# Attention, a dense MoE and a routed MoE on one core: joint attention bursts, earlier weight requests, another order of the last routing, and VectorE on both weight halves of three experts

## Chip, core and metric

The kernel runs on one core of a Trainium2 chip. The metric is the device time of one execution in microseconds; the median of the runs is compared. The inputs are drawn at random from a fixed seed.

## What is computed

Three stages follow each other. `x` passes from one to the next.

```
# 1. chunked attention, 4 x 8 heads, 768 positions, head size 64; per chunk of 32 positions
k_full = concat(mem_k (8), k[16 left .. 8 right]);  v_full likewise
out[chunk] = softmax(q[chunk] @ k_full.T / 8) @ v_full
# 2. dense MoE block on 3072 tokens of 512
g = x @ w_gate;  x = (silu(g) * (x @ w_val)) @ w_out          # 512 -> 1536 -> 512
# 3. routed MoE, 8 experts, top 1
e = argmax(x @ w_gate2);  p = softmax(x @ w_gate2)[e];  o = sigmoid(x @ w_output_gate)[e]
out = p * o * (relu(x @ w1[e]) @ w2[e])                       # 512 -> 1024 -> 512
```

The dense weights of stage 2 come as 64-bit floats and are converted on the chip; the rest is 32-bit.

## The kernel before

**Tiles.** The 3072 tokens are 8 token groups of 384. A token group is 6 attention tiles of 64 positions (48 tiles in all). A program counter, not a scheduler, sets the order: the order in which the code is written is the order of each engine's queue.

**Attention as pieces.** `attention_pieces` lists small steps: `at_T` transposes queries or keys of a tile, `at_S` scores one tile, `at_S2` scores two tiles (from tile 14, `PAIRED`, on), `at_N` normalises, `at_PT` transposes probabilities, `at_PV` multiplies with the values of one tile and writes `xh` and its remainder `xl`. The pieces of token group g+1 are spread over the 36 slots of token group g (`slot`, `run_pieces`). Most pieces take a buffer of the PSUM pool `ps_a`, a ring of three.

**The dense block.** For each of 12 column blocks f of a token group, TensorE does 12 matmuls for the gate (`m1_gate`), 12 for the value (`m1_val`) and 9 for the output of the block before (`m1_out`). Every operand is split in a high and a low part, which gives three passes for each product. `split_gv` and `split_o` make the parts of the weights for each token group anew: ScalarE copies the high one, GpSimd subtracts for the low one.

**Conversion.** In token group 0 the 36 weight pieces of 512 KB are loaded on SyncE's queue into `wst`, and converted by two ScalarE steps (`conv_act`), three VectorE steps and a GpSimd add (`conv_dve`). Seven are begun in the attention of token group 0, the others about one in a slot. `wst` has two buffers of three pieces each, and `conv_rest` asks for the piece three ahead.

**Routing.** After a token group `m1_done` puts its routing steps in a list with delays in slots (`later`, `tick`): `rt_T` transposes, `rt_L` logits, `rt_M` and `rt_1` the choice, `rt_2` the positions, `rt_3` the write of the rows, `rt_R` the scatter of token numbers into a table by GpSimd. The last token group also makes the schedule of the experts, 14 steps of very small VectorE work, one in each tick.

**Experts.** Steps 0 to 2 (`NEARLY`) serve three experts with 256 tokens each, steps 3 on are read from the schedule. Each step has 8 chunks of hidden columns: `mm1` (12 matmuls), relu on ScalarE and its remainder `h` on VectorE, `mm2` one chunk later. `split_chunk` splits the two weights of a chunk two chunks ahead: ScalarE copies both high parts, VectorE subtracts for the first weight, GpSimd for the second. There are two ticks in a chunk. Rows of tokens are gathered by GpSimd (`gather`) with indices that SyncE reads from the table (`load_idx`).

## Time and profile before

| | |
|---|---|
| median of 3 runs | 1137.72 us (1136.55 to 1138.33) |
| the profiled execution | 1136.55 us, span 1134.8 us |
| TensorE busy | 1088.2 us, 96% |
| VectorE, ScalarE, GpSimd busy | 607.1, 595.6 and 667.7 us |
| chain that ended last | TensorE 82%, VectorE 6%, DMA 3%, GpSimd 3% |

The span is that of the profiler's records, and 1.75 us lie around it. Busy shares are averages over stages with different limits: attention of token group 0 up to 42 us, token groups 0 to 7 up to 788 us, then the experts. A busy TensorE says little by itself, since a matmul that starts late inside a run of matmuls is also counted.

### The profile page before, as it was taken

The numbers are of one execution on the slowest core, as the hardware profiler recorded it, in microseconds if no ns is written. First come the engines' busy times: TensorE is split into PE (matmuls) and PEld (weight loads), VectorE is DVE, ScalarE is ACT, GpSimd is POOL, SyncE is SP. The second block draws the span as 40 slices with busy tenths as digits, with TensorE's granted clock in tenths as the row PEclk, the third lists the DMA queues.
The fourth block names the chain that finished last, engine by engine and source line by source line (L and its number), as shares of the span: only waits on it lengthen the run. The fifth ranks groups of instructions, "written<-read, shape, count | busy, mean of one in ns | idle before, by whom it ended". The sixth has DMA issues, their size and how long they took to land.

```text
span 1134.8 us, 20274 instructions
## 1 busy us (share of the span) xinstructions
PE 1088.2 (96%) x7268; PEld 967.5 (85%) x7268; DVE 607.1 (53%) x1260; ACT 595.6 (52%) x1336; POOL 667.7 (59%) x459
## 2 busy tenths in 40 slices
PE   7889899999999999999999999999989999999994
PEld 5778788898898999889889899998769988888883
DVE  6799954544444544544444443334786344444563
ACT  5678755545556555555554554444535344445551
POOL 4589854554654554464455465566547566666773
PEclk7799999999999999999999999999999999999997
DMA  8776624301211220221130010254319655555774
GB/s 218 191 201 206 180 69 123 54 22 36 65 38 38 59 46 23 59 44 31 45 59 22 8 42 1 75 104 149 120 54 336 226 175 179 187 173 192 223 233 127
DMA packets 204574, 125.73 MB, mean 111 GB/s; under 512 B 110768, under 2 KB 181552, under 8 KB 204466
## 3 DMA queue, kind: packets, MB, share of 16 engines
q1 hardware_dynamic: 199282, 110.70, 35.6%
q0 software_dynamic: 5184, 13.66, 3.5%
q8 instruction: 59, 0.97, 0.4%
q14 instruction: 49, 0.40, 0.1%
HBM read 110.82 MB, written 14.04 MB: 110 GB/s over the span
## 4 chain that ended last, share of the span: by engine, by line
PE 82%; DVE 6%; DMA 3%; POOL 3%; issue 2%; ACT 2%; SPq 0%; POOLq 0%; ACTq 0%; DVEq 0%
PE ps_g L533 33%; PE acc L574 16%; PE g L1036 12%; PE o L1071 11%; PE ps_pv L436 2%; PE ps_t L328 2%; PE ps_att L419 2%; PE ps_att L389 1%; DMA st<-in_moe_w_gate_dram 1%; DMA st<-in_moe_w_val_dram 1%; PE ps_x L620 1%; PE a L1022 1%; POOL gvl L183 1%; DVE ps_c L231 1%; DVE ps_c L229 1%
## 5 line engine op out<-in xcount | busy, mean ns | idle before, releaser
L183 POOL TENSOR_TENSOR gvl<-w,gvh 128x1024 fp32r<-128x1024 f32 x96 | 233.6, 2434 | 89.2 <-ACT gvh L182 60.6
L533 PE MATMUL ps_g<-xh,gvh 128*128 128x384 f32 x768 | 270.3, 352 | 0.6 <-ACT gvh L182 0.6
L533 PE MATMUL ps_g<-xh,gvl 128*128 128x384 f32 x768 | 259.5, 338 | 2.4 <-POOL gvl L183 2.4
L533 PE MATMUL ps_g<-xl,gvh 128*128 128x384 f32 x768 | 259.4, 338 | 0.0
L183 POOL TENSOR_TENSOR ol<-w,oh 128x512 fp32r<-128x512 f32 x96 | 124.4, 1295 | 197.6 <-ACT oh L182 197.5
L574 PE MATMUL acc<-oh,h 128*128 128x512 f32 x576 | 202.0, 405 | 0.0
L546 DVE SCALAR_TENSOR_TENSOR th<-th,ps_g 128x384 f32<-128x384 f32 x96 | 53.0, 552 | 185.8 <-ACT th L541 183.1
L533 PEld LDWEIGHTS ps_g<-xh,gvh 128*128 128x128 f32 x768 | 144.9, 189 | 5.2 <-ACT gvh L182 0.8
L533 PEld LDWEIGHTS ps_g<-xh,gvl 128*128 128x128 f32 x768 | 144.6, 188 | 3.5 <-POOL gvl L183 3.5
L533 PEld LDWEIGHTS ps_g<-xl,gvh 128*128 128x128 f32 x768 | 145.1, 189 | 1.9
L557 ACT CAST h<-th 128x384 fp32r<-128x384 f32 x96 | 49.2, 512 | 165.6 <-DVE th L555 165.5
L574 PEld LDWEIGHTS acc<-oh,h 128*128 128x128 f32 x576 | 108.2, 188 | 27.6 <-issue 4.4
L574 PE MATMUL acc<-ol,h 128*128 128x512 f32 x288 | 113.8, 395 | 0.3 <-POOL ol L183 0.3
L1046 ACT ACTIVATE h<-g 128x256 fp32r<-128x256 f32 (+2 forms) x96 | 36.0, 375 | 146.2 <-PE g L1036 134.0
L563 DVE TENSOR_TENSOR h<-th,h 128x384 fp32r<-128x384 f32 x96 | 82.8, 862 | 40.0 <-ACT h L557 40.0
L182 ACT CAST gvh<-w 128x1024 fp32r<-128x1024 f32 x96 | 100.4, 1047 | 1.9 <-POOL w L237 1.8
L541 ACT ACTIVATE th<-ps_g 128x384 f32<-128x384 f32 x96 | 47.0, 489 | 91.2 <-PE ps_g L533 91.0
L1048 DVE SCALAR_TENSOR_TENSOR h<-g,h 128x256 fp32r<-128x256 f32 (+2 forms) x96 | 39.4, 410 | 95.5 <-ACT h L1046 41.5
L555 DVE TENSOR_TENSOR th<-th,ps_g 128x384 f32<-128x384 f32 x96 | 53.0, 552 | 58.2 <-PE ps_g L533 56.5
L972 POOL TENSOR_TENSOR wl<-w,wh 128x512 fp32r<-128x512 f32 x30 | 49.4, 1648 | 35.4 <-ACT wh L970 32.2
L1071 PE MATMUL o<-gvh,h 128*128 128x512 f32 x184 | 66.3, 399 | 4.1 <-DVE h L1048 4.1
L972 POOL TENSOR_TENSOR gvl<-w,gvh 128x512 fp32r<-128x512 f32 x30 | 46.9, 1563 | 37.8 <-ACT gvh L970 36.3
(252 smaller groups left out, 2344.3 us busy)
## 6 DMA issues: line engine op xcount, KB each, us to landing
w<-in_moe_w_dram SPq DMA_DIRECT2D x120, 256.0 KB
ra<-in_moe_w_dram SPq DMA_DIRECT2D x72, 256.0 KB
kt<-in_k_dram SPq DMA_DIRECT2D x35, 176.0 KB
vt<-in_v_dram SPq DMA_DIRECT2D x35, 176.0 KB
xs<-xr SPq DMA_DIRECT2D x8, 769.5 KB
st<-in_moe_w_gate_dram SPq DMA_DIRECT2D x12, 512.0 KB
st<-in_moe_w_val_dram SPq DMA_DIRECT2D x12, 512.0 KB
st<-in_moe_w_out_dram SPq DMA_DIRECT2D x12, 512.0 KB
```

The costliest lines, as they stand in the source:

```text
L182: nc.scalar.copy(out=hi, in_=src)
L183: lo_eng.tensor_tensor(out=lo, in0=src, in1=hi.bitcast(F32), op=ALU.subtract)
L533: nc.tensor.matmul(ps, a[:, c], x[:, kk, :], start=(n == 0), stop=(n == 3 * KD - 1))
L541: nc.scalar.activation(out=th, in_=ps, func=AF.Tanh, scale=0.5)
L546: nc.vector.scalar_tensor_tensor(out=th, in0=th, scalar=1.0, in1=ps, op0=ALU.add, op1=ALU.mult)
L555: nc.vector.tensor_tensor(out=hh, in0=hh, in1=ps, op=ALU.mult)
L557: nc.scalar.copy(out=h1, in_=hh)
L563: nc.vector.tensor_tensor(out=h2, in0=hh, in1=h1.bitcast(F32), op=ALU.subtract)
L574: nc.tensor.matmul(accs[g][j], a[:, c], w_, start=(f == 0 and n == 0), stop=(f == NF - 1 and n == 2))
L972: eng.tensor_tensor(out=b[:, i], in0=r[:, i], in1=a[:, i].bitcast(F32), op=ALU.subtract)
L1036: nc.tensor.matmul(ps, wx[:, 0, c * P:(c + 1) * P], xx[:, c, :], start=(i == 0), stop=(i == 3 * KD - 1))
L1071: nc.tensor.matmul(ysd[s][t][0:hx.shape[1]], hx, wx[:, 1], start=(j == 0 and i == 0), stop=(j == NFE - 1 and i == len(passes) - 1))
```

## The change

There are five edits.

- Loads: `wst` has six buffers of one piece each, and from the second conversion on `conv_rest` asks for the piece five ahead.
- Attention: the values of two tiles are multiplied in one piece (`at_PV2`), and from tile 12 on together with the scores of the next two tiles (`at_PVS`). Mask and exponentials of the second of these tiles are a piece of their own (`at_X`). The transposes of tile 6 move from the attention ahead of token group 0 into its slots.
- Routing: the steps get other delays, in successive slots for the last two token groups, and later ones for the others. The schedule's 14 steps come at ticks 10 to 29 instead of 13 to 26.
- A memset of one number for each partition goes ahead of each of the last token group's three scatters.
- For the 24 chunks of the first three experts VectorE does both subtractions of a split.

```diff
@@ -91,7 +92,7 @@
     s_wst = ctx.enter_context(ExitStack())
     ldp = s_att.enter_context(tc.tile_pool(name="ldp", bufs=2))
     ap2 = s_att.enter_context(tc.tile_pool(name="ap2", bufs=2))
-    wst = s_wst.enter_context(tc.tile_pool(name="wst", bufs=2, side="right"))
+    wst = s_wst.enter_context(tc.tile_pool(name="wst", bufs=NST, side="right"))
...
         if W64:
-            dst, cast = staged[f].rearrange("p c t -> p (c t)"), lambda a: a.bitcast(I32)
+            staged[f, j] = wst.tile([P, KD * P, 2], I32, tag="st", name="st")
+            dst, cast = staged[f, j].rearrange("p c t -> p (c t)"), lambda a: a.bitcast(I32)
         else:
-            dst, cast = wres[f], lambda a: a
-        n = KD * P * (2 if W64 else 1)
-        dst = dst[:, j * n:(j + 1) * n]
+            dst, cast = wres[f][:, j * KD * P:(j + 1) * KD * P], lambda a: a
...
-        st = staged[f][:, j * KD * P:(j + 1) * KD * P, :]
+        st = staged.pop((f, j))
...
     def conv_rest():
         nonlocal n_conv
-        if n_conv >= 3:
-            load_w(*divmod(n_conv + 3, 3))
+        if n_conv > 0:
+            load_w(*divmod(n_conv + NST - 1, 3))
         conv_dve()
         n_conv += 1
...
         for z in range(2):
-            s = ap2.tile([P, HP, CTXM], F32, tag="s", name="s", bufs=3)
-            mx = sm.tile([P, HP, 1], F32, tag="mx", name="mx")
-            nc.vector.tensor_tensor(out=s, in0=ps[z], in1=mk, op=ALU.add)
-            nc.vector.tensor_reduce(out=mx, in_=s, axis=AX.X, op=ALU.max, negate=True)
-            den = dens[(i + z) % 3]
-            for j in range(HP):
-                nc.scalar.activation(
-                    out=s[:, j, :], in_=s[:, j, :], func=AF.Exp,
-                    bias=mx[:, j, :], accum_out=den[:, j, 0:1])
-            probs[i + z] = (s, den)
+            score[i + z] = ps[z]
+
+    def at_X(i):
+        t = i % NT // 2 * 2
+        mi = 3 if t == 0 else (4 if t == NT - 2 else 0)
+        mk = masks[:, mi:mi + 1, :].to_broadcast([P, HP, CTXM])
+        s = ap2.tile([P, HP, CTXM], F32, tag="s", name="s", bufs=3)
+        mx = sm.tile([P, HP, 1], F32, tag="mx", name="mx")
+        nc.vector.tensor_tensor(out=s, in0=score.pop(i), in1=mk, op=ALU.add)
+        nc.vector.tensor_reduce(out=mx, in_=s, axis=AX.X, op=ALU.max, negate=True)
+        den = dens[i % 3]
+        for j in range(HP):
+            nc.scalar.activation(
+                out=s[:, j, :], in_=s[:, j, :], func=AF.Exp,
+                bias=mx[:, j, :], accum_out=den[:, j, 0:1])
+        probs[i] = (s, den)
...
+    def at_PV2(i):
+        g, tt = divmod(i, GU)
+        if g not in xT:
+            xT[g] = (xp.tile([P, KD, GT], F32R, tag="xh", name="xh"),
+                     xp.tile([P, KD, GT], F32R, tag="xl", name="xl"))
+        xh, xl = xT[g]
+        ps = ps_a.tile([P, HP, 2 * QT], F32, tag="a", name="ps_pv")
+        for u in range(2):
+            vt = vals.pop(i + u)
+            for h in range(H):
+                z = h % 2
+                nc.tensor.matmul(
+                    ps[z * D:z * D + D, h // 2, u * QT:u * QT + QT], vt[:, h, :],
+                    pT[i + u][:, h // 2, z * QT:z * QT + QT] if i < PAIRED
+                    else pT[i + z][:, h // 2, u * QT:u * QT + QT],
+                    start=True, stop=True)
+        dst = (slice(None), slice(None), slice(tt * QT, (tt + 2) * QT))
+        load_v(i + 3)
+        load_v(i + 4)
+        copy_out(i < 2 * GU, xh[dst], ps)
+        nc.vector.tensor_tensor(out=xl[dst], in0=ps, in1=xh[dst].bitcast(F32), op=ALU.subtract)
+
+    def at_PVS(i):
+        at_PV2(i)
+        if i + 2 < NTT:
+            at_S2(i + 2)
+            at_X(i + 2)
+
...
-            if n < GU and n + 1 >= done_t:
+            if n < GU - 1 and n + 1 >= done_t:
...
-        for n in range(GU, NTT + 2):
-            if n < PAIRED:
-                yield at_T, (n + 1, 0)
-                yield at_T, (n + 1, 1)
-            if GU <= n - 3 < PAIRED:
-                yield at_PV, (n - 3,)
-            if n < PAIRED:
-                yield at_S, (n,)
-            if GU <= n - 2 < PAIRED:
+        yield at_T, (GU, 0)
+        yield at_T, (GU, 1)
+        for n in range(GU, PAIRED):
+            yield at_T, (n + 1, 0)
+            yield at_T, (n + 1, 1)
+            if n % 2 == 0 and n - 4 >= GU:
+                yield at_PV2, (n - 4,)
+            yield at_S, (n,)
+            if n - 2 >= GU:
                 yield at_PT, (n - 2,)
-            if n <= PAIRED and n - 1 >= GU:
+            if n - 1 >= GU:
                 yield at_N, (n - 1,)
-            if n == PAIRED - 1:
+        yield at_PV2, (PAIRED - 4,)
...
+        yield at_PT, (PAIRED - 2,)
+        yield at_N, (PAIRED - 1,)
+        yield at_PT, (PAIRED - 1,)
+        for n in range(PAIRED, NTT + 2, 2):
+            if n > PAIRED:
+                yield at_PT, (n - 2,)
+                yield at_PT, (n - 1,)
+            if n + 2 < NTT:
+                yield at_T, (n + 2, 0)
+            yield at_PVS, (n - 2,)
+            if n < NTT:
+                yield at_X, (n + 1,)
+                yield at_N, (n,)
+            if n + 2 < NTT:
                 yield at_T, (n + 2, 1)
-            if n < PAIRED:
-                continue
-            even = n % 2 == 0
-            if even:
-                if n - 2 >= PAIRED:
-                    yield at_PT, (n - 2,)
-                    yield at_PT, (n - 1,)
-                if n < NTT:
-                    yield at_S2, (n,)
-            else:
-                if n < NTT:
-                    yield at_N, (n - 1,)
-                if n - 3 >= PAIRED:
-                    yield at_PV, (n - 3,)
-                if n < NTT:
-                    yield at_N, (n,)
+            if n < NTT:
+                yield at_N, (n + 1,)
             if n + 2 < NTT:
-                for w in range(n % 2, 2):
-                    yield at_T, (n + 2, w)
-            if not even and n - 3 >= PAIRED:
-                yield at_PV, (n - 2,)
+                yield at_T, (n + 3, 1)
...
-        if fn_p is at_PV:
+        if fn_p is at_X:
+            ends[(args_p[0] - 3) // GU] = n_p + 1
+        if fn_p in (at_PV, at_PV2, at_PVS):
             ends[args_p[0] // GU] = n_p + 1
...
+        t_T, t_L, t_M, t_1, t_2, t_3 = (
+            ((1, 2, 3), 4, 5, 6, 9, 8) if g >= NG - 2 else ((2, 4, 6), 11, 12, 13, 16, 15))
         for j in range(GJ):
-            later(2 + 2 * j, rt_T, st, j)
-        later(8, rt_L, st)
-        later(9, rt_M, st)
-        later(10, rt_1, st)
-        later(13, rt_2, st, g)
-        later(12, rt_3, st, g)
+            later(t_T[j], rt_T, st, j)
+        later(t_L, rt_L, st)
+        later(t_M, rt_M, st)
+        later(t_1, rt_1, st)
+        later(t_2, rt_2, st, g)
+        later(t_3, rt_3, st, g)
...
+        if g == NG - 1:
+            gap = sm.tile([P, 1], F32, tag="gap", name="gap", bufs=1)
+            nc.gpsimd.memset(gap, 0.0)
...
-        for i, eng in enumerate((nc.vector, nc.gpsimd)):
+        low = (nc.vector, nc.vector if n < NEARLY * NFE else nc.gpsimd)
+        for i, eng in enumerate(low):
             eng.tensor_tensor(
                 out=b[:, i], in0=r[:, i], in1=a[:, i].bitcast(F32), op=ALU.subtract)
...
         sched = make_schedule()
         for i in range(14):
-            later(13 + i, next, sched, None)
+            later(10 + 3 * i // 2, next, sched, None)
```

On TensorE, in token group 1, the first scores of two tiles before (`ps_att` is the scores' buffer, `acc` and `ps_g` the dense block's):

```order
L574 MATMUL acc_768<-oh,h_1815 128x512
L574 MATMUL acc_768<-ol,h_1815 128x512
L574 MATMUL acc_768<-oh,h_1826 128x512
L389 MATMUL ps_att<-kT,qbd_116 64x96 x16
L533 MATMUL ps_g<-xh,gvh 128x384
L533 MATMUL ps_g<-xl,gvh 128x384
L533 MATMUL ps_g<-xh,gvl 128x384
```

and in the change (`ps_pv` is the values' buffer, `ps_x` that of a routing transpose):

```order
L562 MATMUL ps_g<-xh,gvl 128x384
L459 MATMUL ps_pv<-pT,vt 64x64 x16
L384 MATMUL ps_att<-kT,qbd_116 64x96 x16
L651 MATMUL ps_x<-ident,xr 128x128 x4
L562 MATMUL ps_g<-xh,gvh 128x384
L562 MATMUL ps_g<-xl,gvh 128x384
```

The scores now stand right behind the values of two tiles, and here a routing transpose stands right behind both.

On VectorE, at the start of the schedule, before (`xi` to `t` are rows of the schedule, `h` the remainder of a chunk's result, `wl` and `gvl` low parts of weights, `xl` that of tokens):

```order
L746 SCALAR_TENSOR_TENSOR xi<-base,ebase 1x8
L740 TENSOR_SCALAR ho<-xi 1x8 x3
L776 CAST hof<-ho 1x24
L1048 SCALAR_TENSOR_TENSOR h_9083<-g,h_9082 128x256
L972 TENSOR_TENSOR wl<-w,wh 128x512
L644 TENSOR_TENSOR hf<-hof,early_110 1x8
L746 SCALAR_TENSOR_TENSOR t_9093<-hf,hof 1x8
L644 TENSOR_TENSOR t_9095<-t_9093,hof 1x8
L644 TENSOR_TENSOR t_9093<-t_9093,t_9095 1x8
```

and in the change:

```order
L1083 SCALAR_TENSOR_TENSOR h_8973<-g,h_8972 128x256
L1007 TENSOR_TENSOR gvl<-w,gvh 128x512 x2
L780 SCALAR_TENSOR_TENSOR xi<-base,ebase 1x8
L774 TENSOR_SCALAR ho<-xi 1x8 x3
L810 CAST hof<-ho 1x24
L184 TENSOR_TENSOR xl<-a,xh 128x4x128
L675 TENSOR_TENSOR hf<-hof,early_110 1x8
L780 SCALAR_TENSOR_TENSOR t_9007<-hf,hof 1x8
L675 TENSOR_TENSOR t_9009<-t_9007,hof 1x8
```

Each chunk now has two subtractions of weights on VectorE, and fewer steps of the schedule stand between two results.

On SyncE's queue, at the first load for tile 6, before (`qt`, `kt` are queries and keys of an attention tile, `st` is a weight piece):

```order
L290 DMA qt<-in_q_dram 128x8x64
L274 DMA kt<-in_k_dram 88x8x64
L277 DMA kt<-in_mem_k_dram 8x8x64
L206 DMA st<-in_moe_w_gate_dram 128x4x256
L274 DMA kt<-in_k_dram 88x8x64
L277 DMA kt<-in_mem_k_dram 8x8x64
L206 DMA st<-in_moe_w_val_dram 128x4x256
```

and in the change:

```order
L204 DMA st<-in_moe_w_gate_dram 128x4x256
L204 DMA st<-in_moe_w_val_dram 128x4x256
L288 DMA qt<-in_q_dram 128x8x64
L272 DMA kt<-in_k_dram 88x8x64
L275 DMA kt<-in_mem_k_dram 8x8x64
L202 DMA st<-in_moe_w_out_dram 128x1024
```

Two weight pieces moved ahead of tile 6's queries and keys.

## Rows read from the trace of the kernel before

**Rows 1.** Busy time by stage: window, its length; PE, PEld, DVE, ACT, POOL (instructions), clock, DMA, GB/s.
```profile
41.00:140.00 99.00, 87.39 (x558) 77.10 (x554) 86.59 (x156) 74.99 (x174) 84.39 (x61) 0.97 0.70 195
...
368.00:460.00 92.00, 92.00 (x680) 82.58 (x679) 43.78 (x92) 50.22 (x126) 48.92 (x29) 1.00 0.20 44
```

**Rows 2.** ScalarE in order of time, start: start us, length us, instruction.
```profile
35.90 1.19 ACT L315 ACTIVATE qbd<-ps_t 64x512 f32<-64x512 f32 x2
```

**Rows 3.** Waits of ScalarE, 42 to 140 us: total us, times, longest.
```profile
ACT ps_c L220 <- DMA st<-in_moe_w_gate_dram: 4.3, 3, 2.1
```

**Rows 4.** TensorE in order of time, token group 2: start us, length us.
```profile
372.28 0.60 PE L419 MATMUL ps_att<-ident,s 128*96 128x128 f32 x4
372.63 0.42 PE L533 MATMUL ps_g<-xh,gvh 128*128 128x384 f32 x1
372.90 0.34 PE L533 MATMUL ps_g<-xl,gvh 128*128 128x384 f32 x1
373.07 0.34 PE L533 MATMUL ps_g<-xh,gvl 128*128 128x384 f32 x1
...
374.67 0.34 PE L533 MATMUL ps_g<-xh,gvl 128*128 128x384 f32 x1
374.93 0.89 PE L389 MATMUL ps_att<-kT,qbd 64*64 64x96 f32 x32
375.75 0.50 PE L574 MATMUL acc<-oh,h 128*128 128x512 f32 x1
376.10 0.39 PE L574 MATMUL acc<-ol,h 128*128 128x512 f32 x1
376.33 0.62 PE L574 MATMUL acc<-oh,h 128*128 128x512 f32 x2
```

**Rows 5.** A value burst and its subtraction, TensorE and VectorE in order of time.
```profile
413.09 0.69 PE L436 MATMUL ps_pv<-pT,vt 96*64 96x64 f32 x16
...
415.12 0.42 DVE L445 TENSOR_TENSOR xl<-ps_pv,xh 128x256 fp32r<-128x256 f32 x1 [1.37 <-ACT xh L319]
```

**Rows 6.** First expert product, line 1036, by window: length, PE busy (matmuls), PEld busy, clock.
```profile
814.00:846.00 32.00, 13.04 (x90) 11.94 (x88) 0.95 0.13 42
846.00:861.00 15.00, 7.77 (x61) 7.61 (x60) 1.00 0.88 281
```

**Rows 7.** GpSimd and VectorE in order of time, first experts.
```profile
822.89 1.28 POOL L972 TENSOR_TENSOR gvl<-w,gvh 128x512 fp32r<-128x512 f32 x1 [3.02 <-ACT gvh L970]
...
822.99 1.20 DVE L746 SCALAR_TENSOR_TENSOR sh<-sh,tri__9146 1x8 f32<-1x8 f32 x1
```

**Rows 8.** VectorE's busy time in one window: length, busy (instructions), clock, DMA, GB/s.
```profile
806.00:843.00 37.00, 33.55 (x123) 0.95 0.10 36
```

**Rows 9.** VectorE's groups, 806 to 843 us: busy us, mean ns, idle before.
```profile
L972 DVE TENSOR_TENSOR wl<-w,wh 128x512 fp32r<-128x512 f32 x4 | 5.2, 1309 | 0.2 <-ACT wh L970 0.2
L1048 DVE SCALAR_TENSOR_TENSOR h<-g,h 128x256 fp32r<-128x256 f32 x9 | 3.7, 407 | 0.6 <-ACT h L1046 0.6
L972 DVE TENSOR_TENSOR gvl<-w,gvh 128x512 fp32r<-128x512 f32 x4 | 2.7, 675 | 0.5 <-ACT gvh L970 0.5
...
L740 DVE TENSOR_SCALAR li<-sidx,used 1x9 f32<-1x9 f32 x1 | 1.3, 1251 | 0.0
...
L701 DVE SCALAR_TENSOR_TENSOR xr<-ot,se 128x3 f32<-128x3 f32 x1 | 1.0, 1001 | 0.0
...
L740 DVE TENSOR_SCALAR li<-sidx,q__9174 1x10 f32<-1x10 f32 x1 | 0.2, 213 | 0.0
```

**Rows 10.** Waits of SyncE's queue and of TensorE, 740 to 880 us.
```profile
SPq L988 <- DMA table<-tokid,posi: 3.1, 1, 3.1
...
PE ps_g L533 <- POOL gvl L183: 2.0, 1, 2.0
```

**Rows 11.** SyncE's queue and GpSimd in order of time, step 3 of the experts.
```profile
843.77 1.65 SPq L988 DMA_DIRECT2D idx<-table  x2
...
852.24 0.99 POOL L1000 DMA_INDIRECT xg<-xs,idx  x1 [0.15 <-DMA w<-in_moe_w_dram]
```

More of the change, by code (lines that the diff above doesn't have):

```diff
@@ L71, in tile_chunk_attention_moe_moe2 @@
     NCV = 6
+    NST = 6
     PAIRED = 2 * GU + 2
@@ L194, in load_w @@
             wres[f] = wrp.tile([P, 3 * KD * P], F32, tag="w", name="w")
-            if W64:
-                staged[f] = wst.tile([P, 3 * KD * P, 2], I32, tag="st", name="st")
         if W64:
-            dst, cast = staged[f].rearrange("p c t -> p (c t)"), lambda a: a.bitcast(I32)
-        else:
-            dst, cast = wres[f], lambda a: a
-        n = KD * P * (2 if W64 else 1)
-        dst = dst[:, j * n:(j + 1) * n]
+            staged[f, j] = wst.tile([P, KD * P, 2], I32, tag="st", name="st")
+            dst, cast = staged[f, j].rearrange("p c t -> p (c t)"), lambda a: a.bitcast(I32)
+        else:
+            dst, cast = wres[f][:, j * KD * P:(j + 1) * KD * P], lambda a: a
         if j == 2:
@@ L260, in split_o @@
         hi_lo(wres[f][:, 2 * KD * P:], *wo[f], nc.gpsimd)
-    first, loaded, vals, qkT, probs, pT, xT = {}, {}, {}, {}, {}, {}, {}
+    first, loaded, vals, qkT, probs, pT, xT, score = {}, {}, {}, {}, {}, {}, {}, {}
     def load_win(tl, src, mem, i):
@@ L379, in at_S2 @@
     def at_S2(i):
-        t = i % NT
-        mi = 3 if t == 0 else (4 if t == NT - 2 else 0)
-        mk = masks[:, mi:mi + 1, :].to_broadcast([P, HP, CTXM])
         qT = qkT.pop((i, 0))
@@ L471, in attention_pieces @@
                 yield at_T, (t, 1)
-        for n in range(GU, NTT + 2):
-            if n < PAIRED:
-                yield at_T, (n + 1, 0)
-                yield at_T, (n + 1, 1)
-            if GU <= n - 3 < PAIRED:
-                yield at_PV, (n - 3,)
-            if n < PAIRED:
-                yield at_S, (n,)
-            if GU <= n - 2 < PAIRED:
+        yield at_T, (GU, 0)
[7 more added lines that the diff above has]
+            if n - 2 >= GU:
                 yield at_PT, (n - 2,)
-            if n <= PAIRED and n - 1 >= GU:
+            if n - 1 >= GU:
                 yield at_N, (n - 1,)
-            if n == PAIRED - 1:
-                yield at_T, (n + 2, 1)
-            if n < PAIRED:
-                continue
-            even = n % 2 == 0
-            if even:
-                if n - 2 >= PAIRED:
-                    yield at_PT, (n - 2,)
-                    yield at_PT, (n - 1,)
-                if n < NTT:
-                    yield at_S2, (n,)
-            else:
-                if n < NTT:
-                    yield at_N, (n - 1,)
-                if n - 3 >= PAIRED:
-                    yield at_PV, (n - 3,)
-                if n < NTT:
-                    yield at_N, (n,)
+        yield at_PV2, (PAIRED - 4,)
+        yield at_T, (PAIRED + 1, 1)
+        yield at_PT, (PAIRED - 2,)
[12 more added lines that the diff above has]
+            if n + 2 < NTT:
+                yield at_T, (n + 2, 1)
+            if n < NTT:
+                yield at_N, (n + 1,)
             if n + 2 < NTT:
-                for w in range(n % 2, 2):
-                    yield at_T, (n + 2, w)
-            if not even and n - 3 >= PAIRED:
-                yield at_PV, (n - 2,)
+                yield at_T, (n + 3, 1)
     pieces = list(attention_pieces())
```

## The prediction

> **What bounds the kernel now.** I read the busy times by stage first. In the steady part, token groups 1 to 6, TensorE is busy 92.00 of 92 us while VectorE, ScalarE and GpSimd stand near half [rows 1]. There only TensorE's own work, and the cost of breaking its stream, is worth anything. In token group 0 it is busy 87.39 of 99 us, with VectorE at 86.59 and GpSimd at 84.39 [rows 1]: conversion of the weights, which those two carry, shares the limit with the loads behind it. The waits of ScalarE show the loads: its first conversion step waits 4.3 us in three places for a gate weight [rows 3].
>
> The third place is the start of the routed experts. From 814 to 846 us TensorE does 90 matmuls of the first expert product, 7.5 chunks of 12; in the 15 us behind that it does 61, 5.1 chunks at 2.95 us with their share of transposes [rows 6]. At that pace 7.5 chunks fill 22.1 of the 32 us, so 9.9 us are lost. VectorE is the reason: between 806 and 843 us it is busy 33.55 of 37.0 us [rows 8], and the idle time ahead of its large groups is 0.2, 0.6 and 0.5 us [rows 9]; I count some 2 us as idle and the other 35 as work, with the gaps between small instructions.
>
> **The change part by part.** All sums are against the profiled execution, 1136.55 us (span 1134.8 and 1.75 around it). It lies 1.17 us below the median, 1137.72.
>
> *Start.* The transposes of tile 6 leave the attention of token group 0. With them go two ScalarE copies, 1.19 us together [rows 2], which stand ahead of the conversion that the first weight split waits for behind VectorE and GpSimd. That is on the path to the first dense matmul; I take -1.2, ends 0 (another engine's step is late anyway) and -2 (VectorE's key copy leaves too). The copies come back in the first slots.
>
> *Weights asked five ahead.* Each of the six buffers is now free by itself, and a load goes out two conversions earlier. Two conversions are two slots, over 5 us, more than any of the waits, of which the longest is 2.1 us [rows 3]. The 4.3 us should go, but VectorE has only 12.4 us of idle time in that stage [rows 1], about half of it before its first conversion there. I take -3.0, ends 0 (VectorE and GpSimd are the limit) and -5.6 (the waits for other weights go too). Queued behind a weight load on SyncE's queue are the key and value windows; two weight loads now stand ahead of tile 6's query and keys, and wait for the first two conversions. Tile 6 itself is needed later than before, which covers it; without that cover it would cost one load, under 4 us.
>
> *Joint bursts.* A burst of 64-wide matmuls in the dense stream costs a gap at entry, 374.93 - 374.67 = 0.26 against a spacing of 0.17, and one at exit, 376.10 - 375.75 = 0.35 against 0.23: 0.21 us in all [rows 4]. A burst of transposes costs only its exit, 0.27 against 0.17: 0.10 us [rows 4]. By the order, the 36 value bursts and 17 score bursts of tiles 12 to 47 become 18 bursts: 18 joins of value with value, 17 of value with score. Transposes stand alone 13 times more. The value joins save 18 x 0.21 = 3.8 us. The join of value with score changes the shape, from 96x64 to 64x64, in the middle of the burst; it saves between 0 and 3.6 us, and I take half, 1.8. Less 1.3 us for the transposes, that is -4.3.
>
> The rows show the gap at both ends of a burst but not between two shapes inside one. The Trainium skill (TensorEngine Tiling (Array Packing), Key Properties) states that a change of the tiling mode, though not of the tile, drains TensorE. By that the middle keeps an entry of about 0.1 us, and the term would be -4.5 (an estimate with that page) instead of -4.3; the gaps of [rows 4] agree with it.
>
> *A wait that the joint burst adds.* It takes all three buffers of ps_a in a row: one for two tiles' values, two for scores. Whoever comes next in the ring gets the buffer of the values, and waits for its copy and subtraction. Today that buffer is free at 415.12 + 0.42 = 415.54, and the burst ends its issue some 0.6 us after 413.09 [rows 5]: about 1.84 us. Twice the width adds some 0.5 us, so 2.3, of which the scores cover 0.8. By the order 2 of the 17 bursts (both in token group 1) are followed at once by a routing step that needs the buffer: 2 x 1.5 = +3.0. In the other 15 at least nine dense matmuls, 2.1 us, lie between. The ends are 0 and +8 (a few of the 15 wait too). So the steady part gives -1.3, ends -6 and +4.
>
> *Routing of the last two token groups.* The list of token positions is written four slots earlier. SyncE's load of the indices waited 3.1 us for it, GpSimd's gather for that load, the split behind the gather for GpSimd, and TensorE 2.0 us for the split [rows 10]. With the list there, what is late next is ScalarE's weight copy, at no cost seen. I take -2.0, ends 0 and -2.3. The three tiny memsets are GpSimd's, which has time there.
>
> *Splits to VectorE, schedule spread out.* In 24 chunks GpSimd's half of the split goes to VectorE, and the 14 schedule steps take 20 half-slots instead of 14. Added to VectorE: 0.6 us a chunk (a group of four splits without a stall averages 675 ns, the next instruction begins some 0.07 earlier) [rows 9]. Removed: what VectorE loses to GpSimd. A step on 8 numbers begins at 822.99, lasts 1.20 us and ends within 0.02 us of GpSimd's split, 822.89 + 1.28 [rows 7]. Seven small steps between 806 and 843 take 1.00 to 1.25 us (the longest and the shortest are in [rows 9]) where the twin of the longest takes 0.21 [rows 9]; that is about 6.7 us. Four wl splits average 1309 against 675 ns: 2.5 more [rows 9]. So of the 35 us, 9.2 are waits for GpSimd. Without them 25.8 remain; 9 second halves (one per result instruction, of which there are 9 [rows 9]) add 5.4; the same small steps now lie over some 11.5 chunks, so 2.5 more chunks, of 0.4 + 2 x 0.6 = 1.6 us each, add 4.0: 35.2 us, against 11.5 x 2.95 = 33.9 on TensorE. VectorE is still slightly the longer, but TensorE needs a chunk's result only one chunk later. I take 2 us of the 9.9 as left.
>
> The experts of step 3 come sooner after the schedule: its indices were asked at 843.77 and gathered at 852.24 [rows 11], with GpSimd busy until then, and used at 861; after the change the schedule ends some 11 us before that use. A late gather costs 0 to 2 us; I take 1. This part is -7.0, ends -9 (all of the loss) and +1 (the waits for GpSimd stay, so VectorE needs 44.4 us for 33.9).
>
> A rule that speaks against more VectorE time here: a gather issue on GpSimd takes 0.99 us [rows 11], and the Trainium skill (SBUF — State Buffer, section SBUF: two separate sides, its box on the trap for GpSimd's DMAs) states that while VectorE runs in a two-port mode GpSimd cannot write its descriptors. The split is a plain two-input subtraction, which that page does not count among such modes; were it one, three gathers would each lose up to a split of 0.67 us, and the part would be -5 instead of -7. No run so far shows it.
>
> **Sum.** -1.2 - 3.0 - 1.3 - 2.0 - 7.0 = -14.5. From 1136.55 that is 1122.05, and on the median 1123.2; I say 1123.
>
> **The rivals.**
> 1. *Splits only change place.* The long VectorE steps are not GpSimd's doing, and the part gives +1: 1131. For it: VectorE is the late engine and gets work. Against: the ends that coincide [rows 7].
> 2. *More comes free.* The buffer wait is covered, the first conversions start sooner and the experts lose nothing: start -2, weights -5, bursts -4.3, routing -2, experts -9, together -22: 1115. For it: the long idle stretch of VectorE when group 0 begins. Against: two conversion engines at 87 and 85 percent.
> 3. *The ring of ps_a becomes the limit.* The joint burst holds all three buffers, and ScalarE's copy of the values can stand behind one of its weight copies. If the 15 other bursts also wait, each us costs 15; from 1.0 us each the whole gain is gone, and at 1.5 us the time is 1123 + 22 = 1145, slower. Against: 2.1 us of dense work and 0.8 us of scores cover 2.3.
> 4. *Prefetch does nothing and gathers come late.* Group 0 stays, step 3 costs 4 us and half of the 15 bursts wait 0.5: 1123 + 4.2 + 3 + 3.8 = 1134 to 1137, no change.
>
> **How the numbers follow.** Forecast 0.64 (1118 to 1129), rival 1 0.10, rival 2 0.17, rival 3 0.04, rival 4 0.05. The predicted time is the forecast's, 1123. The range runs from 1112 to 1132: it takes in rivals 1 and 2 and most ends of single terms, and leaves about 0.12 out. A change under 0.2%, 2.3 us, is about what a measurement cannot tell from none. Faster by more than that: 0.92; within it: 0.04; slower: 0.04.
>
> **What would show it.** In the profile after: joint value and score bursts with one gap at each end; two waits of a routing step for the subtraction of values in token group 1 and none elsewhere; ScalarE hardly waiting for weights; no wait of 2 us for a split ahead of the routed experts; VectorE's small schedule steps at 0.13 to 0.3 us, and its splits in pairs at 0.67. Wrong would be: TensorE waits in every joint burst, small steps still over 1 us, or a wait for the gathered rows of step 3 above 2 us.

## The result and the profile after

The changed kernel takes 1112.53 us (median of 4 runs, 1112.31 to 1112.67); the kernel before, run beside it, 1138.03 (4 runs, 1136.55 to 1140.34). The ratio is 0.9774, with a 95% interval of 0.9757 to 0.9791. The span of the profiled execution fell from 1134.8 to 1110.5 us. The forecast of 1123 is 10 us too slow; 1112.5 lies at the low end of the range, nearest to rival 2 (more comes free).

Where the 24.3 us went is read from these starts: TensorE's first dense matmul, ScalarE's first gate activation of token groups 1 and 7, and TensorE's first matmul of the first expert and of step 3. The early experts are the first three, 24 chunks:

| us | to the first dense matmul | group 0 | groups 1 to 6 | group 7 | early experts | the rest |
|---|---|---|---|---|---|---|
| before | 41.92 | 113.20 | 550.70 | 82.24 | 82.78 | 263.96 |
| after | 40.95 | 109.54 | 542.34 | 79.39 | 74.40 | 263.88 |
| difference | -1.0 | -3.7 | -8.4 | -2.9 | -8.4 | -0.1 |
| forecast | -1.2 | -3.0 | -1.3 | -2.0 | -7.0 | 0 |

In five kernels that share the code of after in groups 1 to 6 these take 542.3 to 542.4 us, and in eight that share its experts the early ones take 74.2 to 74.4. But before and b_split (below), which share their code in groups 1 to 6, take 550.70 and 549.83 there, in every group a little apart and at no single wait; the cause is open. The first two columns repeat less well: in five kernels with the code of after up to group 1, their sum lies between 149.1 and 150.8 us (before, and a kernel that shares its code there: 155.1 and 155.4). About -5.2 is the better number for them, against a forecast of -4.2.

Busy time of after in the windows of [rows 1] and [rows 8], with the same columns:

```profile
41.00:140.00 99.00, 91.05 (x568) 80.97 (x569) 88.76 (x156) 78.16 (x183) 86.42 (x62) 0.97 0.69 190
368.00:460.00 92.00, 92.00 (x690) 83.93 (x689) 41.34 (x90) 51.33 (x123) 49.31 (x31) 1.00 0.19 44
806.00:843.00 37.00, 36.61 (x235) 32.12 (x236) 30.75 (x89) 18.65 (x30) 5.27 (x5) 1.00 0.43 135
```

In group 0 TensorE gained 3.7 us of busy time. In the steady window it is full as before, but holds 690 matmuls instead of 680. Among the experts GpSimd stands almost still (5.27 of 37 us), and TensorE is nearly full. All waits of ScalarE between 42 and 140 us (total, times, longest) hold no weight load any more, where [rows 3] had 4.3 us of waits for gate weights:

```profile
ACT h L586 <- DVE th L584: 11.2, 9, 3.0
ACT th L570 <- PE ps_g L562: 5.1, 1, 5.1
ACT s L372 <- DVE mx L369: 2.3, 3, 1.5
ACT gvh L183 <- POOL w L235: 1.6, 3, 0.7
ACT qbd L313 <- PE ps_t L326: 0.4, 1, 0.4
```

All waits of TensorE between 142 and 600 us, and then between 780 and 850 us:

```profile
PE ps_x L651 <- DVE xl L468: 0.6, 1, 0.6
PE ps_r L710 <- DVE xl L468: 0.6, 1, 0.6
```
```profile
PE o L1106 <- DVE h L1083: 1.4, 3, 0.5
```

These are the two buffer waits forecast for token group 1, at 0.6 us each, and what is left among the experts. A joint burst of after on TensorE in order of time (start, length):

```profile
349.76 0.34 PE L562 MATMUL ps_g<-xh,gvl 128*128 128x384 f32 x1
350.03 1.15 PE L459 MATMUL ps_pv<-pT,vt 96*64 96x64 f32 x32
351.11 0.89 PE L384 MATMUL ps_att<-kT,qbd 64*64 64x96 f32 x32
351.93 0.50 PE L603 MATMUL acc<-oh,h 128*128 128x512 f32 x1
352.27 0.39 PE L603 MATMUL acc<-ol,h 128*128 128x512 f32 x1
```

Start to start: values 351.11 - 350.03 = 1.08, scores 351.93 - 351.11 = 0.82. The scores took 375.75 - 374.93 = 0.82 alone as well [rows 4]: between the two shapes no gap is seen. VectorE's groups of after, 806 to 843 us, answer to [rows 9]:

```profile
L1083 DVE SCALAR_TENSOR_TENSOR h<-g,h 128x256 fp32r<-128x256 f32 x13 | 5.4, 412 | 3.1 <-ACT h L1081 1.9 <-issue 1.2
...
L1007 DVE TENSOR_TENSOR wl<-w,wh 128x512 fp32r<-128x512 f32 x8 | 5.1, 672 | 0.0
L1007 DVE TENSOR_TENSOR gvl<-w,gvh 128x512 fp32r<-128x512 f32 x6 | 3.8, 672 | 0.0
```

A split takes 672 ns where `wl` took 1309, and 13 results come in 37 us where 9 did.

### The profile page after: what moved, and what is told of

Read it like the earlier page. It is cut to its first block, busy times and chain, and to the rows that moved or that the text cites. A ratio compares the mean times of both kernels' runs of the same rounds, so it can differ in the third digit from the quotient of the medians.

```text
span 1110.5 us, 20227 instructions
## 1 busy us (share of the span) xinstructions
PE 1075.1 (97%) x7268; PEld 966.2 (87%) x7268; DVE 585.0 (53%) x1260; ACT 594.6 (54%) x1318; POOL 630.5 (57%) x438
## 4 chain that ended last, share of the span: by engine, by line
PE 81%; DVE 11%; issue 3%; POOL 2%; ACT 1%; DMA 1%; SPq 0%; POOLq 0%; ACTq 0%; DVEq 0%
PE ps_g L562 32%; PE acc L603 16%; PE g L1071 11%; PE o L1106 11%; PE ps_pv L459 2%; PE ps_t L326 2%; DVE ps_c L229 2%; DVE w L232 2%; DVE ps_c L227 2%; PE ps_att L420 2%; PE ps_att L384 1%; PE ps_x L651 1%; PE a L1057 1%; POOL gvl L184 1%; PE ps_l L659 1%
## 5 line engine op out<-in xcount | busy, mean ns | idle before, releaser
L184 POOL TENSOR_TENSOR gvl<-w,gvh 128x1024 fp32r<-128x1024 f32 x96 | 230.4, 2401 | 98.8 <-ACT gvh L183 97.2
L184 POOL TENSOR_TENSOR ol<-w,oh 128x512 fp32r<-128x512 f32 x96 | 125.6, 1309 | 181.8 <-ACT oh L183 151.8
L592 DVE TENSOR_TENSOR h<-th,h 128x384 fp32r<-128x384 f32 x96 | 64.1, 668 | 31.2 <-ACT h L586 31.2
L1106 PE MATMUL o<-wh,h 128*128 128x512 f32 x184 | 65.8, 396 | 0.9 <-DVE h L1083 0.9
L399 ACT ACTIVATE s<-s,mx 128x96 f32<-128x96 f32 x136 | 49.4, 364 | 32.0 <-DVE mx L396 31.9
```

The lines of the kernel that those rows point to most:

```text
L184: lo_eng.tensor_tensor(out=lo, in0=src, in1=hi.bitcast(F32), op=ALU.subtract)
L399: nc.scalar.activation(out=s[:, j, :], in_=s[:, j, :], func=AF.Exp, bias=mx[:, j, :], accum_out=den[:, j, 0:1])
L592: nc.vector.tensor_tensor(out=h2, in0=hh, in1=h1.bitcast(F32), op=ALU.subtract)
L1106: nc.tensor.matmul(ysd[s][t][0:hx.shape[1]], hx, wx[:, 1], start=(j == 0 and i == 0), stop=(j == NFE - 1 and i == len(passes) - 1))
```

## The experiments

Each kernel is the changed one with one thing altered, unless it says otherwise. Ratios are to the kernel before, run on the same chip.

### The joint bursts

**u_att** has the attention pieces of before (tile 6 too), with the routing delays of before for token groups 0 to 5.

```diff
-        for n in range(PAIRED, NTT + 2, 2):
...
-            yield at_PVS, (n - 2,)
+        for n in range(GU, NTT + 2):
...
+                if n - 3 >= PAIRED:
+                    yield at_PV, (n - 3,)
...
-            ((1, 2, 3), 4, 5, 6, 9, 8) if g >= NG - 2 else ((2, 4, 6), 11, 12, 13, 16, 15))
+            ((1, 2, 3), 4, 5, 6, 9, 8) if g >= NG - 2 else ((2, 4, 6), 8, 9, 10, 13, 12))
```

> The changed kernel with the attention pieces of the kernel before, and the routing delays of token groups 0 to 5 as before; loads, splits, schedule and the last two routings stay changed. Theory 1 (the joins themselves save: 0.35 us for each of 18 joins of value with value, 0.21 us for each of 17 joins of value with score, less 1.3 us for lone transposes): token groups 1 to 6 take 550 us again instead of 543, and the whole is 7 to 8 us slower than the changed kernel, some 1120 us. Theory 2 (the 7 us come from the other routing delays or from the earlier weights, which also let those token groups run freer): less than 3 us slower, some 1113 to 1115 us.

Measured: 1125.75 us (1124.68 to 1126.33), ratio 0.9888 (0.9871 to 0.9904). Groups 1 to 6 take 549.83 us, 7.5 more than after: the joins, with the routing delays that go with them, are worth that much. The whole is 5.8 us above the 1120 of theory 1, since the start grew too. A burst of one tile's values there, TensorE in order of time:

```profile
329.17 0.34 PE L531 MATMUL ps_g<-xh,gvl 128*128 128x384 f32 x1
329.43 0.69 PE L434 MATMUL ps_pv<-pT,vt 96*64 96x64 f32 x16
330.05 0.50 PE L572 MATMUL acc<-oh,h 128*128 128x512 f32 x1
330.39 0.40 PE L572 MATMUL acc<-ol,h 128*128 128x512 f32 x1
```

16 matmuls take 0.62 us; 32 in one burst take 1.08. So 16 more cost 0.46, and each burst has 0.16 us of its own inside, beside the gaps at its ends. Two bursts of one tile cost 2 x (0.62 + 0.21) = 1.66, one of two tiles 1.08 + 0.21 = 1.29: 0.37 saved for each join.

The start grew by 5.8 us, to 46.73. TensorE's longest wait there (total, times, longest):

```profile
PE ps_t L326 <- DMA qt<-in_q_dram: 2.6, 1, 2.6
```

With tile 6 back on the path to the first dense matmul, its queries stand behind the two weight pieces in SyncE's queue. The prediction named moving tile 6 as the cover of that, and under 4 us as its price without. Against before, which has tile 6 in the start as well, the start is 4.8 us longer, so the price was higher; 2.6 of it are seen as a wait for the queries.

**sep_s2** keeps the values of two tiles joint, but makes the scores a piece of their own behind them.

```diff
-        if i + 2 < NTT:
-            at_S2(i + 2)
-            at_X(i + 2)
+    def at_S2X(i):
+        at_S2(i)
+        at_X(i)
...
             yield at_PVS, (n - 2,)
             if n < NTT:
+                yield at_S2X, (n,)
                 yield at_X, (n + 1,)
```

> The changed kernel, with the scores of two tiles as a piece of their own behind the piece with the values: the two stand apart in nearly all pairs. Theory 1 (a change of the matmul's shape inside a burst costs nothing, so this join saves its full 0.21 us): 17 x 0.21 = 3.6 us slower than the changed kernel, less up to 1.2 us for the two buffer waits if these go, so 1115 to 1116 us. Theory 2 (the shape change costs a gap inside the joint burst too, as a drain would): about 2 us or less slower, 1113 to 1114 us.

Measured: 1113.59 us (1112.95 to 1114.02), ratio 0.9785 (0.9769 to 0.9801), which times alone can't tell from after. By stage they differ: groups 1 to 6 take 543.79 us, 1.45 more. Group 1 became 0.6 shorter, since its two buffer waits are covered, and the five others longer. 1.45 + 1.2 of waits = 2.65 for 17 joins, 0.16 each. That is a net price: by the order of its trace ten bursts of sep_s2 are followed at once by transposes or routing matmuls, where in after two are, so 8 gaps fewer stand against the 17 joins. At 0.10 for each of them, the exit of transposes, a join is worth by this estimate (2.65 + 0.8) / 17 = 0.20, about the two gaps of 0.21. The rest of u_att's loss, 549.83 - 543.79 = 6.0 us, is the value joins: 0.34 for each of 18, what the transposes cost already taken off. Values alone, TensorE in order of time:

```profile
405.14 0.40 PE L605 MATMUL acc<-oh,h 128*128 128x512 f32 x1
405.47 1.15 PE L459 MATMUL ps_pv<-pT,vt 96*64 96x64 f32 x32
406.55 0.45 PE L564 MATMUL ps_g<-xh,gvh 128*128 128x384 f32 x1
406.84 0.34 PE L564 MATMUL ps_g<-xl,gvh 128*128 128x384 f32 x1
```

They take 406.55 - 405.47 = 1.08, the same as ahead of scores, with an exit gap of 0.29 against 0.17. The join saves this exit and the scores' entry, and pays nothing in the middle that can be seen. The Trainium skill (TensorEngine Tiling (Array Packing), Key Properties) states that a change of the tiling mode drains TensorE. If 96x64 and 64x64 are two modes, which no run here shows, the drain between them is too short to be seen.

**abut** moves the third routing transpose one slot earlier and the positions one later, so that in groups 2 to 5 too a routing step stands right behind a joint burst: 8 more places.

```diff
-            ((1, 2, 3), 4, 5, 6, 9, 8) if g >= NG - 2 else ((2, 4, 6), 11, 12, 13, 16, 15))
+            ((1, 2, 3), 4, 5, 6, 9, 8) if g >= NG - 2 else ((2, 4, 5), 11, 12, 13, 17, 15))
```

> The changed kernel with two routing delays of token groups 0 to 5 altered (the third transposes one slot earlier, the positions one slot later), so that routing matmuls stand right behind eight more joint bursts. Theory 1 (the wait for the buffer of the values is 0.6 us wherever a user of the ring follows at once): 8 x 0.6 = 5 us slower than the changed kernel, less 8 x 0.1 for the bursts that are saved, 1116 to 1117 us. Theory 2 (the prediction's price, 1.5 us each): 11 us slower, 1123 us. Theory 3 (the waits are covered): no slower than the changed kernel, 1112 us.

Measured: 1119.79 us (1119.39 to 1120.26), ratio 0.9838 (0.9821 to 0.9854); groups 1 to 6 take 549.70, 7.4 more. Group 1 is 0.5 us shorter, so the 8 places cost 7.9, 1.0 each. All waits of TensorE from 142 to 700 us, and one of the places in order of time, TensorE and ScalarE:

```profile
PE ps_x L651 <- DVE xl L468: 4.7, 5, 1.0
PE ps_r L710 <- DVE xl L468: 4.1, 4, 1.0
```
```profile
353.16 0.89 PE L384 MATMUL ps_att<-kT,qbd 64*64 64x96 f32 x32
355.06 0.66 PE L651 MATMUL ps_x<-ident,xr 128*128 128x128 f32 x4 [1.02 <-DVE xl L468]
```
```profile
353.19 0.61 ACT L183 CAST oh<-w 128x512 fp32r<-128x512 f32 x1
353.71 0.58 ACT L317 CAST xh<-ps_pv 128x512 fp32r<-128x512 f32 x1
```

The mechanism of rival 3 is real, down to its detail: ScalarE's copy of the values stands behind a copy of a weight (`oh`). In group 1 of after it doesn't, and the wait is 0.6. Where the routing steps stand decides the matter: with the delays of abut all the gain of the joins would have gone. In group 1 abut is faster than after (90.91 against 91.45 us), since one of the two waits there is gone.

### The weight loads

**u_loads** has the two buffers of three pieces of before, asked three ahead.

```diff
-    wst = s_wst.enter_context(tc.tile_pool(name="wst", bufs=NST, side="right"))
+    wst = s_wst.enter_context(tc.tile_pool(name="wst", bufs=2, side="right"))
...
-        if n_conv > 0:
-            load_w(*divmod(n_conv + NST - 1, 3))
+        if n_conv >= 3:
+            load_w(*divmod(n_conv + 3, 3))
```

> The changed kernel with the weight buffers and requests of the kernel before (two buffers of three pieces, three ahead). Theory 1 (the earlier requests gave token group 0 its 3.5 us): the first dense matmul still at 41 us, token group 0 back to 112 us, the whole 3 to 4 us slower than the changed kernel, 1116 us. Theory 2 (VectorE and GpSimd are the limit in token group 0, and the 3.5 us come from the joint value pieces and the tile that moved): within 1 us of the changed kernel, 1112 to 1113.5 us, though ScalarE waits some 4 us for weights again.

Measured: 1118.89 us (1118.64 to 1119.9), ratio 0.9833 (0.9817 to 0.985). Start and group 0 together take 156.7 us, 5.9 to 7.6 more than the five kernels with early loads. ScalarE waits for weights again, 42 to 142 us (the lines left out are waits for other engines). Then group 0 of u_loads and of after, with the columns of [rows 1]:

```profile
ACT ps_c L221 <- DMA st<-in_moe_w_val_dram: 6.3, 2, 3.4
...
ACT ps_c L221 <- DMA st<-in_moe_w_gate_dram: 0.9, 1, 0.9
```
```profile
41.83:156.71 114.88, 103.89 (x651) 92.58 (x652) 92.65 (x162) 82.46 (x188) 94.59 (x66) 0.95 0.61 169
```
```profile
40.95:150.49 109.54, 101.59 (x651) 90.59 (x652) 93.45 (x162) 81.94 (x189) 94.46 (x66) 0.97 0.64 176
```

The waits, 7.2 us, are about what the loads cost. VectorE and GpSimd are busy for nearly as long, but VectorE is idle for 114.88 - 92.65 = 22.2 us instead of 109.54 - 93.45 = 16.1. TensorE's clock is a little lower too, 0.95 against 0.97; what that adds wasn't separated. Against before and b_split (155.1 and 155.4) the kernel is 1.3 to 1.6 us slower there. The work of tile 6, which came into group 0, may be the reason; one execution, in a part whose sum varies by 1.7 us, does not show it.

**st5** has five buffers and asks four ahead.

```diff
-    NST = 6
+    NST = 5
-    LOADS = "w0 q0 q1 q2 w1 v0 v1 q3 w2 q4 w3 w4 v2 w5 q5 v3 v4 v5"
+    LOADS = "w0 q0 q1 q2 w1 v0 v1 q3 w2 q4 w3 w4 v2 q5 v3 v4 v5"
```

> The changed kernel with five weight buffers instead of six, each piece asked four conversions ahead instead of five; the sixth piece is no longer asked ahead of the first slots. Theory 1 (lead time is what the loads lacked): one conversion less of lead is some 2.7 us, and with three ahead in two shared buffers ScalarE waited 7.2 us in three places, the longest 3.4; so at four ahead a part of a wait comes back: token group 0 takes 1 to 3 us more than the 109.5 of the changed kernel. Theory 2 (buffers that come free one by one are what mattered, and VectorE and GpSimd are the limit from then on): token group 0 stays within 0.7 us of the changed kernel's, and no wait of ScalarE for a weight piece is listed.

Measured: 1112.32 us (1111.96 to 1112.52), ratio 0.9768 (0.9743 to 0.9792): no slower than after. One wait of ScalarE for a weight came back (2.2 us, an output weight), and group 0 takes 110.04. The wait goes with the first theory, the time of group 0 with the second. Start and group 0 together take 150.80 us, at the upper end of the five kernels (149.1 to 150.8), so a cost of 1 us or less can't be excluded. Whether single buffers or the one conversion more of lead made the gain wasn't separated.

### The experts and the routing

**u_split** gives GpSimd its half of the splits back.

```diff
-        low = (nc.vector, nc.vector if n < NEARLY * NFE else nc.gpsimd)
+        low = (nc.vector, nc.gpsimd)
```

> The changed kernel with GpSimd's half of the weight splits of the first three experts back on GpSimd; schedule and routing stay spread out as changed. Theory 1 (the lost time was VectorE waiting for GpSimd, some 9 us of its 35): the small schedule steps take 1.0 to 1.25 us again where they meet a GpSimd split, the first 24 chunks take 79 to 81 us instead of 74.4, the whole 5 to 6 us slower than the changed kernel, 1118 us. Theory 2 (the spread of the schedule over more chunks gave the 8.4 us): small steps long again, but covered, at most 2 us slower, 1113 to 1114.5 us.

Measured: 1118.78 us (1118.14 to 1119.31), ratio 0.982 (0.979 to 0.9851). The early experts take 82.19 us, 7.8 more. Two small steps of VectorE and a split of GpSimd in order of time, from two views, and then TensorE's wait:

```profile
796.98 0.15 DVE L675 TENSOR_TENSOR t<-t,hof 1x8 f32<-1x8 f32 x1
797.16 1.19 DVE L675 TENSOR_TENSOR t<-t,t 1x8 f32<-1x8 f32 x1
```
```profile
797.08 1.25 POOL L1007 TENSOR_TENSOR wl<-w,wh 128x512 fp32r<-128x512 f32 x1
```
```profile
799.11 1.22 PE L1106 MATMUL o<-gvh,h 128*128 128x512 f32 x2 [3.02 <-DVE h L1083]
```

A product of 8 numbers takes 1.19 us and ends at 798.35, GpSimd's split at 798.33, as in [rows 7]. The step just ahead, on as many numbers but begun before that split, takes 0.15. TensorE's waits for `h` in this stage are 6.9 us in all, instead of 1.4, and the clock behind the longest of them costs another 1.7 (last section). The Trainium skill (SBUF — State Buffer, section SBUF: two separate sides) states that VectorE with two inputs in SBUF and GpSimd reading it exclude each other for a whole instruction. The trace agrees, and shows the long time also on a step that takes one tensor and a single number (`li`, 1251 ns in [rows 9], 210 in after).

**u_sched** puts the schedule's steps back to ticks 13 to 26.

```diff
-            later(10 + 3 * i // 2, next, sched, None)
+            later(13 + i, next, sched, None)
```

> The changed kernel with the 14 schedule steps at ticks 13 to 26 as in the kernel before; both halves of the splits stay on VectorE and the routing stays early. Theory 1 (waits for GpSimd were the cause): VectorE has about 1.6 us of chunk work and 2 us of schedule in each of 7 chunks against 2.9 on TensorE, so some 4 to 5 us over in that stretch, of which a chunk of slack covers 2: 2 to 3 us slower than the changed kernel, 1115 us, all of it in the first 24 chunks. Theory 2 (the spread is what counts): 6 us or more slower, 1118 us or more.

Measured: 1113.99 us (1112.92 to 1114.01), ratio 0.9774 (0.9744 to 0.9804). The early experts take 75.93 us, 1.5 more; TensorE's waits for `h` are 2.8 us instead of 1.4.

**b_split** is the kernel before with VectorE on both halves, and with the memset of the change.

```diff
-        for i, eng in enumerate((nc.vector, nc.gpsimd)):
+        for i, eng in enumerate((nc.vector, nc.vector if n < NEARLY * NFE else nc.gpsimd)):
```

> The kernel before with only VectorE doing both halves of the splits for the first three experts (and the memset ahead of the last three scatters). Theory 1: VectorE loses its waits for GpSimd, 9 us, and gains 5.4 us of work in the stretch of the schedule, so the first 24 chunks take 78 to 80 us instead of 82.8: 1134 us. Theory 2 (VectorE is simply the fullest engine there, and work added to it adds time): the first 24 chunks take 86 to 90 us, 1141 to 1145 us.

Measured: 1133.7 us (1132.21 to 1135.2, 10 runs), ratio 0.9948 (0.9935 to 0.9961). The early experts take 78.27 us, 4.5 less than before; token group 7 takes 83.78, 1.5 more, though its code up to the wait there is that of before (the wait is 2.5 us here, and the clock fell behind it). So the stage of the early experts falls in steps: 82.78 before, 78.27 with the splits, 75.93 with the routing of the last groups in successive slots (u_sched, which also has the change's loads and bursts, but these end before this stage), 74.40 with the schedule spread. Without the splits the other two bring only 0.6 (82.19): they pay once VectorE is free of GpSimd. The memset alone wasn't tried.

**u_rt6** gives the routing of token group 6 its delays of before.

```diff
-            ((1, 2, 3), 4, 5, 6, 9, 8) if g >= NG - 2 else ((2, 4, 6), 11, 12, 13, 16, 15))
+            ((1, 2, 3), 4, 5, 6, 9, 8) if g >= NG - 1 else ((2, 4, 6), 8, 9, 10, 13, 12)
+            if g == NG - 2 else ((2, 4, 6), 11, 12, 13, 16, 15))
```

> The changed kernel with the routing of token group 6, which runs in token group 7, at the delays of the kernel before. Theory 1 (the early list of positions removed the 2.3 us wait for a split in token group 7): that wait is back, token group 7 takes 81.6 us instead of 79.4, the whole 2.3 us slower than the changed kernel, 1115 us. Theory 2 (the wait went because GpSimd has no expert split to do and is early anyway): token group 7 stays at 79.4 us, no slower than the changed kernel.

Measured: 1116.65 us (1115.61 to 1118.02), ratio 0.9804 (0.9774 to 0.9835). Token group 7 takes 83.80 us, 4.4 more than after. SyncE's wait for the list, TensorE's wait, and busy time around it (columns as in [rows 1]):

```profile
SPq L1024 <- DMA table<-tokid,posi: 4.2, 1, 4.2
```
```profile
PE ps_g L562 <- POOL gvl L184: 2.5, 1, 2.5
```
```profile
754.00:758.00 4.00, 1.78 (x9) 1.19 (x7) 0.56 (x1) 1.95 (x3) 3.67 (x3) 1.00 0.45 140
758.00:762.00 4.00, 3.67 (x13) 3.68 (x14) 0.00 (x0) 0.41 (x1) 3.52 (x5) 0.60 0.36 82
```

The chain of [rows 10] is back. The wait of 2.5 us accounts for part of the 4.4; behind it the granted clock was 0.60 over 4 us, another 4 x 0.4 = 1.6.

### Three tries at a better kernel

**cand1** writes the weight conversions ahead of the attention pieces in the first two slots of token group 0. **cand2** spreads the schedule to ticks 10 to 31 and asks for step 3's rows a chunk later. **cand3** has both, and in token group 1 the routing delays of abut.

```diff
+                if g == 0 and i < 2:
+                    while n_conv < min(3 * NF, NCV + -(-(i + 1) * (3 * NF - NCV) // NSP)):
+                        conv_step()
                 if g + 1 < NG:
...
-            later(10 + 3 * i // 2, next, sched, None)
+            later(10 + 5 * i // 3, next, sched, None)
...
-        ready = 15
+        ready = 16
```

> The changed kernel with one edit: in the first two slots of token group 0 the weight conversions are written ahead of the attention pieces. Theory 1 (conversion, not attention, sets the pace there): the first slots' conversions start sooner, token group 0 takes 0.5 to 1.5 us less. Theory 2 (VectorE and GpSimd stay full either way): within 0.4 us. Rival: tile 6's transposes, now later, make its scores late: 0.5 to 1 us more.

> The changed kernel with the schedule's 14 steps spread further, over ticks 10 to 31 in place of 10 to 29, and the rows of step 3 asked one chunk later. Theory 1 (VectorE is a little short in that stretch, TensorE still waits 2.1 us there for results and splits): 0.4 to 1 us less in the 24 chunks of the first three experts. Theory 2: what is left is not the schedule's, within 0.3 us. Rival: the rows of step 3 come late, 0.5 to 2 us more behind the first three experts.

> Both edits of the two kernels before in one, and in token group 1 alone the third routing transpose one slot earlier and the positions one slot later, so that neither stands right behind a joint burst there. By the run with those delays in all groups, token group 1 takes 0.5 us less (90.9 in place of 91.45) and the two waits of 0.6 us go; with the gains above, 1 to 2.5 us less than the changed kernel in all. Rival: no part can be measured, within 0.5 us.

Measured, on the same chip as st5 (1112.32): cand1 1109.64 us (1108.87 to 1109.82), ratio 0.9746 (0.9721 to 0.977); cand2 1111.84 (1111.21 to 1112.85), 0.9763 (0.9738 to 0.9787); cand3 **1108.98** (1107.48 to 1109.49), 0.9736 (0.9711 to 0.9762). cand1's start and group 0 take 147.3 us, and cand3's, with the same edit, 148.4: both below all five kernels with the order of after. So the conversions set the pace of the first slots, and the gain is larger than expected. cand2 changes nothing (early experts 74.43). cand3 has 90.87 us in group 1, 0.6 less; only the wait of `ps_x` is left. Its median is the lowest of all, some 3 us below st5 and cand2; from cand1 its times can't be told apart.

## Why the prediction was right, and where it was 10 us off

**Start and loads: right, the loads under-sized.** Start and group 0 gave about -5.2 against -4.2. That the start alone came out at -1.0 against -1.2 is luck: the same code takes 40.8 to 41.9 us to the first dense matmul. Its mechanism is in the traces: from ScalarE's last exponential ahead of the first split of weights to the copy for that split it is 4.0 us before (4.4 in b_split), and 2.9 to 3.35 in the five kernels without the two copies. The loads were less well known: asked early they are worth 5.9 to 7.6 us (u_loads), about twice the 3.0 taken and above its far end of 5.6. Another 1.3 to 1.6 us seem to come back with the work of tile 6 in group 0, which I had put at nothing; that this is the cause isn't shown. The step that failed is "VectorE has only 12.4 us of idle time": ScalarE's waits come out as idle time of VectorE behind them, 22.2 us against 16.1, so the whole of the waits goes, not half.

**Joint bursts: right in direction, this term makes most of the miss, 7.1 of 9.8 us.** Forecast -1.3 = -3.8 + 1.3 - 1.8 + 3.0. In its place stand -6.0 for the value joins with the transposes (forecast -2.5), -2.65 for value with score (forecast -1.8), and +1.2 for the ring (forecast +3.0): -7.45. The remaining 0.9 is not the joins': u_att and b_split, whose bursts in these groups are those of before, take 549.83 us both, against 550.70 (cause open, see the result). Two steps failed. I priced a burst by the gaps at its two ends alone, and left out the 0.16 us inside it. And I took the delay of the ring from one burst, [rows 5], whose copy came late: at the two places in after copy and subtraction are over 0.6 us after the scores, not 1.5, and 1.0 where the copy is late (abut). The two places were found right from the order.

**Routing of the last groups: right, but under-sized.** The wait of 2.0 us is gone, and no other took its place. The stage gave -2.9, beyond the far end of -2.3; where the other 0.8 us came from isn't known. u_rt6 shows the mechanism, at 4.4 us: there, and in b_split, the wait is 2.5 us and the clock falls behind it, which the term left out.

**Experts: right, -8.4 against -7.0.** The lock with GpSimd carried it: split pairs at 0.67 us each and small steps at 0.13 to 0.31 us, as forecast. TensorE's waits left are 1.4 us, against 2 taken. The rows of step 3 came in time: asked at 824.21 and gathered from 827.21, here with a pair of splits on VectorE,

```profile
824.21 1.63 SPq L1023 DMA_DIRECT2D idx<-table  x2
```
```profile
827.21 0.99 POOL L1035 DMA_INDIRECT xg<-xs,idx  x1 [23.03 <-DMA idx<-table]
828.50 0.97 POOL L1035 DMA_INDIRECT xg<-xs,idx  x1 [0.30 <-issue]
829.77 0.99 POOL L1035 DMA_INDIRECT xg<-xs,idx  x1 [0.30 <-issue]
```
```profile
828.66 1.29 DVE L1007 TENSOR_TENSOR gvl<-ra,gvh 128x512 fp32r<-128x512 f32 x2 [0.51 <-ACT gvh L1004]
```

so the 1 us kept for a late gather was not needed. The rule weighed against more VectorE time did not bite: the gathers take 0.99, 0.97 and 0.99 us, as before [rows 11], and the second of them lies over the two splits. What I had no term for is the clock. In the rows of before that I read, 0.95 stood beside both windows [rows 6, 8]; smaller windows of before show what it was. TensorE waited 1.86 us for a result, until 816.89, and 0.74 more, until 819.06; then the clock was halved:

```profile
816.89 0.73 PE L1071 MATMUL o<-gvh,h 128*128 128x512 f32 x2 [1.86 <-DVE h L1048]
...
819.06 0.46 PE L1036 MATMUL g<-xh,wl 128*128 128x256 f32 x1 [0.74 <-DVE wl L972]
```
```profile
819.00:820.00 1.00, 0.94 (x5) 0.94 (x6) 0.86 (x7) 0.00 (x0) 0.87 (x1) 0.61 0.00 0
820.00:821.00 1.00, 1.00 (x6) 1.00 (x6) 0.86 (x7) 0.00 (x0) 0.00 (x0) 0.50 0.02 1
```
```profile
818.00:822.00 4.00, 3.26 (x15) 2.96 (x14) 3.72 (x16) 1.32 (x4) 1.70 (x2) 0.65 0.06 19
822.00:826.00 4.00, 3.25 (x19) 2.51 (x18) 3.62 (x20) 1.96 (x3) 2.65 (x3) 0.92 0.00 0
```

The clock was 0.65 from 818 to 822 us and 0.92 from 822 to 826, a shortfall of 4 x 0.35 + 4 x 0.08 = 1.7 us. In after it stays at 1.00, so the early experts got this back besides the waits.

**The rivals.** Rival 1 falls with u_split and b_split. Rival 2 is what happened, for reasons it named only in part. Rival 3's mechanism is shown by abut, at 1.0 us a place, but in after only 2 places had it, at 0.6. Rival 4 falls with u_loads and the gather's times.

## What to carry to other kernels

Price a short burst in a dense stream by its whole length against a burst of twice the work, not by the gaps at its ends. Before joining bursts that drain a buffer ring, list from the order who takes the next buffer: moving two routing steps by one slot decided over 7 us here. Where an engine is full, look first for tiny instructions that take as long as another engine's large one: they are waits, and giving the busy engine more work can make it faster.
